# W_Q loaded in eight transfers of 16 rows, and W_O in four pieces with 20 rows summed early

## The chip, the cores and the metric

The kernel runs on one core of a Trainium2 chip. The metric is the device time of one execution in microseconds. An execution is repeated, and the median of the runs is what is compared. The core has five engines that run side by side: TensorE (matrix products; PE in the profile, with its weight loads shown apart as PEld), VectorE (DVE), ScalarE (ACT), GpSimd (POOL) and SyncE (SP), which here only issues transfers. Transfers between DRAM and the on-chip memory of 128 rows are carried by 16 DMA engines. They go through a queue for each issuing engine: `q1` holds what SP issues, `q10` what ScalarE issues.

## The reference

The reference is one decode step of a transformer block in which attention and the feed-forward part are added up. There are four batch rows, one token each, of 512 values; all arrays are bf16.

```python
x  = A_x                                   # [4, 1, 512]
xn = layernorm(x)
# attention: 32 query heads, 8 key/value heads of 128, window = the last 4096 positions
q  = (xn @ wq).reshape(4, 1, 32, 128)      # wq: [512, 4096]
p  = softmax(q . k / sqrt(128))            # k_cache, v_cache: [4, 8, 16384, 128]
a  = (p @ v).reshape(4, 1, 4096) @ wo      # wo: [4096, 512]
# feed-forward part
b  = (silu(xn @ w_gate) * (xn @ w_up)) @ w_down   # 512 -> 1792 -> 512
return x + a + b
```

What has to be read is the keys and values of the window (8 heads of 4 MB each, twice), W_Q and W_O (4 MB each) and the three feed-forward weights (1.8 MB each): 81 MB in all. Each byte is used for four batch rows only.

## The kernel before, in words

**Transfers.** `run_sync` issues all large transfers from SP, in one fixed order: W_Q, W_gate, W_up, the keys of heads 0 and 1, the values of head 0, then in turn the keys of the next head and the values of the one before, the values of head 7, W_down, and W_O. Each has 128 rows on the chip, and each is one transfer, but for W_O, which goes in five pieces. SP stops ahead of a transfer when the buffer it fills is still in use. There are two buffers for keys (`kbuf`) and two for values (`vbuf`). W_Q lies in the second value buffer until the projection is done, W_down in the buffer of W_gate, and W_O in the first key buffer. ScalarE issues the small transfer of x: four rows of 1 KB.

Row p of W_Q on the chip holds the weight rows 4p to 4p+3, which is 32 KB that lie together in DRAM; the same is true of a row of keys or values. Row p of W_O holds the weight rows 32p to 32p+31; a "row" j of W_O in the list `ROWS` is one of these 32, so that a piece of n such rows is n KB on each of the 128 rows of the chip.

**Head of the kernel** (`t_head` in `run_tensor`). TensorE waits for the layernorm and for W_Q (`d_v[1]`, line 469), makes the query projection in 32 products (lines 470 to 476), transposes it, and makes the gate and up projections as soon as their weights are there. The gated product `guT` is kept for the end.

**A pass for each key/value head** (`t_pass`, eight times). TensorE transposes the keys (line 416); VectorE and ScalarE move them to the on-chip memory; TensorE makes the scores (line 425); then come the maximum, the exponential on ScalarE (line 270), the denominators (line 521) and the product with the values (line 434), one head behind.

**The tail** (`t_tail`). The head outputs are normalised and rearranged into `OP`, which VectorE finishes in lines 384 to 389. Meanwhile TensorE sums the feed-forward part, 14 products with W_down, into the four quarters of one bank, `part_ps` (line 572). It then issues idle products: `spin(4)`, line 574, whose result is not used. Then it adds the first `EARLY` rows of W_O to the same four quarters, one product of 512 columns for each (line 582). VectorE and ScalarE copy the bank to the on-chip memory (lines 391 and 273, 64 rows each). A product with `fold` adds the four quarters into two accumulators of 256 columns each (line 587). The other rows of W_O are added straight to these accumulators, two products for each row (line 593). Two copies make `y` (lines 275 and 393), and SP writes it out (line 253).

TensorE waits for each piece of W_O ahead of the first row of it. In the early part there is a `spin(q)` ahead of that wait for piece q: none for piece 0, one idle product for piece 1. An idle product on fp32 operands shows in the trace as two records of line 442.

What sets the order around the change is the program order on each engine and the semaphores. `d_v[1]` counts the transfers into the second value buffer, W_Q first among them, and later waits count on from there.

Of the kernel before, what the change touches and what calls it, by code (L numbers as in the profile page):

```python
# [10 lines left out]
def bass_parallel_sum__sliding_block_cached__swiglu_ffn__decode_kernel(  # L11
# [31 lines left out]
    SCALE = float(Dh) ** -0.5  # L43
    EPS = 1e-5
    BIG = 1.0e30
    ROWS = [(0, 16), (16, 22), (22, 29), (29, 31), (31, 32)]
    EARLY = 22

    sb = nc.alloc_sbuf_tensor
    sb("pad_to_512", [128, (-nc.sbuf_base) % 512 // 2], BF16)  # L50
# [6 lines left out]
    WQ = VB[1][:].rearrange("p t d -> p (t d)").rearrange("p (c n) -> p c n", c=NC)  # L57
# [66 lines left out]
    def sem(name):  # L124
        return nc.alloc_semaphore(name=name)

    d_x = sem("d_x")
    d_k = [sem("d_k%d" % g) for g in range(2)]
    d_v = [sem("d_v%d" % g) for g in range(2)]
    d_wg = sem("d_wg")  # L130
    d_wu = sem("d_wu")
    d_wd = sem("d_wd")
    d_wo = [sem("d_wo%d" % q) for q in range(len(ROWS))]
    d_out = sem("d_out")
# [42 lines left out]
    wq_ap = A_wq.rearrange("(p c) n -> p c n", c=NC)  # L177
# [7 lines left out]
    def kv_ap(cache, r):  # L185
        return cache[:, r, Sk - W:, :].rearrange("b (s t) d -> s b (t d)", t=NT)

    def bc(ap, n):
        return ap.unsqueeze(1).to_broadcast([ap.shape[0], n, ap.shape[1]])
# [36 lines left out]
    def run_sync(eng):  # L226
        def load_k(r):
            if r >= 2:
                eng.wait_ge(s_tr[NCH - 1], r - 1)
            eng.dma_start(KB[r % 2][:].rearrange("p t d -> p (t d)"), kv_ap(A_k_cache, r)).then_inc(d_k[r % 2], 16)  # L230

        def load_v(r):
            if r:
                eng.wait_ge(s_pv, r)
            eng.dma_start(VB[r % 2][:].rearrange("p t d -> p (t d)"), kv_ap(A_v_cache, r)).then_inc(d_v[r % 2], 16)

        eng.dma_start(WQ[:], wq_ap).then_inc(d_v[1], 16)
        eng.dma_start(WG[:], wg_ap).then_inc(d_wg, 16)
        eng.dma_start(WU[:], wu_ap).then_inc(d_wu, 16)
        load_k(0)  # L240
        load_k(1)
        load_v(0)
        for r in range(2, HKV):
            load_k(r)
            load_v(r - 1)
        load_v(HKV - 1)
        eng.dma_start(WD, wd_ap).then_inc(d_wd, 16)
        for q, (a, b) in enumerate(ROWS):
            if q == 0:
                eng.wait_ge(s_tr[NCH - 1], HKV - 1)  # L250
            eng.dma_start(WO[:, a:b, :], wo_ap[:, a:b, :]).then_inc(d_wo[q], 16)
        eng.wait_ge(s_y, 2)
        eng.dma_start(out_ap, y[:]).then_inc(d_out, 16)
        eng.wait_ge(d_out, 16)
# [140 lines left out]
    def run_tensor(eng):  # L395
# [9 lines left out]
        def step(reg, by, op=ALU.add):  # L405
            nc.regs_alu(reg, reg, by, op=op)
# [32 lines left out]
        def spin(n):  # L439

            for _ in range(n):
                mm(spin_ps, identf[:], bc(o4[:], 2), start=True, stop=True)  # L442
# [13 lines left out]
        with nc.body("t_head", valid_engines=me):  # L456
            loc = eng.mark_branch_hint_location()
            for t, v in ((nx, 1), (odd, 0), (nk[0], 16), (nk[1], 16)):
                nc.regs_mov(t, v)
            eng.wait_ge(s_c2, 1)  # L460
            eng.wait_ge(s_xn, 1)
            for c in range(NC):
                last = eng.transpose(xT_ps[:, c * B:(c + 1) * B],  # L463
                                     xn[:].rearrange("b (p c) -> b c p", c=NC)[:, c, :], ident[0:B, 0:B])
            last.then_inc(s_xT, 1)
            eng.wait_ge(s_const, 1)
            mm(mask_ps, Lsel[:], Dsh[:])
            eng.wait_ge(s_xnT, 1)
            eng.wait_ge(d_v[1], 16)
            for c in range(NC):  # L470
                for j in range(2):
                    for k in range(4):
                        last = mm(ps_S[j][32 * k:32 * k + 32, :], XnT[:, c, :],  # L473
                                  WQ[:, c, 512 * (4 * j + k):512 * (4 * j + k) + 512],
                                  start=(c == 0), stop=(c == NC - 1), skip_group_check=True)
            last.then_inc(s_q, 1)
            eng.wait_ge(s_qs, 2)
            for j in range(2):
                for h in range(4):
                    last = eng.transpose(qT_ps[:, 4 * j + h, :], qs[:, j, 128 * h:128 * h + 128], ident[:])  # L480
            last.then_inc(s_qt, 1)
            for w, d, o, s_w in ((WG, d_wg, gate_ps, s_g), (WU, d_wu, up_ps, s_u)):
                wt = w[:].rearrange("p c (m t) -> p c t m", t=NF)
                eng.wait_ge(d, 16)
                for c in range(NC):
                    for k in range(4):
                        last = mm(o[32 * k:32 * k + 32, :].rearrange("p (t m) -> p t m", m=128), XnT[:, c, :],
                                  wt[:, c, T0[k]:T0[k] + 4, :], start=(c == 0), stop=(c == NC - 1), skip_group_check=True)
                last.then_inc(s_w, 1)
            eng.wait_ge(s_gu, 1)  # L490
            for t in range(4):
                last = eng.transpose(gT_ps[:, t, :], gu[:, 128 * t:128 * t + 128], ident[:])
            last.then_inc(s_gt, 1)
            eng.wait_ge(s_qc, 1)
            eng.wait_ge(s_guT, 1)
            nc.br("t_pass", engines=me)
# [63 lines left out]
        with nc.body("t_tail", valid_engines=me):  # L560
            eng.wait_ge(s_nm, LAST + 2)
            eng.transpose(rt_ps, OT[:, 1:, :].rearrange("p r c -> p (r c)"), ident[:]).then_inc(s_rt, 1)
            eng.wait_ge(s_rn, 1)
            for b in range(B):
                m = mm(op_ps[:, b].rearrange("p q j -> p (q j)"), sel[:, b, :], Rn[:], start=(b == 0), stop=True,
                       skip_group_check=True)
            m.then_inc(s_op, 1)
            eng.wait_ge(s_guT, 1)
            eng.wait_ge(d_wd, 16)
            for t in range(NF):  # L570
                k = (t + 1) % 4
                mm(part_ps[32 * k:32 * k + 32, :], guT[:, t, :], WD[:, t, :], start=(t < 3), stop=False,  # L572
                   skip_group_check=True)
            spin(4)
            eng.wait_ge(s_opc, 1)
            for j in range(EARLY):
                for q, (a, b) in enumerate(ROWS):
                    if a == j:
                        spin(q)
                        eng.wait_ge(d_wo[q], 16)  # L580
                k = (j + 3) % 4
                m = mm(part_ps[32 * k:32 * k + 32, :], OP[:, j, :], WO[:, j, :], start=False,  # L582
                       stop=(j >= EARLY - 4), skip_group_check=True)
            m.then_inc(s_pt, 1)
            eng.wait_ge(s_ptc, 2)
            for h in range(2):
                mm(acc_ps[h], fold[:], part[:, 256 * h:256 * h + 256], start=True, stop=False, skip_group_check=True)
            for j in range(EARLY, 32):
                for q, (a, b) in enumerate(ROWS):
                    if a == j:  # L590
                        eng.wait_ge(d_wo[q], 16)
                for h in range(2):
                    m = mm(acc_ps[h], OP[:, j, :], WO[:, j, 256 * h:256 * h + 256],  # L593
                           start=False, stop=(j == 31), skip_group_check=True)
            m.then_inc(s_acc, 1)
            step(seen, 1)
            eng.br_lt(seen, 1, on_true="t_tail", on_false="t_end").branch_hint(loc)
        nc.switch_bb("t_end")

    run_gpsimd(nc.gpsimd)  # L600
    run_sync(nc.sync)
    run_scalar(nc.scalar)
    run_vector(nc.vector)
    run_tensor(nc.tensor)


# [26 lines left out]
```

## Time and profile before

| | |
|---|---|
| median of 3 runs | 196.24 us (196.23 to 196.3) |
| the profiled execution's own time | 196.33 us |
| its span, first to last instruction | 195.0 us |
| moved by DMA | 81.09 MB, mean 416 GB/s |
| busy share of TensorE / VectorE / ScalarE | 81% / 59% / 35% |
| mean granted TensorE clock | 0.965 |

The page gives the share of the span in which each engine was busy, and a row of digits with the busy share in each of 40 slices (4.9 us each). The line "DMA" does the same for the 16 DMA engines together, and "GB/s" gives what they moved. The chain of waits is followed back from the last instruction, each step to what released it. A view by windows gives, for any stretch of time, the busy time of each engine, the granted clock, the share of DMA and the rate. In it the time and the bytes of a packet are put down to the window in which it begins, so that in a short window the share can be over 1. One packet is one row of a transfer, or the few bytes that report the end of one DMA engine's part.

### The profile page before, as it was taken

The numbers are of one execution on the slowest core, as the hardware profiler recorded it, in microseconds if no ns is written. First come the engines' busy times: TensorE is split into PE (matmuls) and PEld (weight loads), VectorE is DVE, ScalarE is ACT, GpSimd is POOL, SyncE is SP. The second block draws the span as 40 slices with busy tenths as digits, with TensorE's granted clock in tenths as the row PEclk, the third lists the DMA queues.
The fourth block names the chain that finished last, engine by engine and source line by source line (L and its number), as shares of the span: only waits on it lengthen the run. The fifth ranks groups of instructions, "written<-read, shape, count | busy, mean of one in ns | idle before, by whom it ended". The sixth has DMA issues, their size and how long they took to land.

```text
span 195.0 us, 6476 instructions
## 1 busy us (share of the span) xinstructions
PE 158.2 (81%) x2889; PEld 123.0 (63%) x2898; DVE 115.5 (59%) x220; ACT 69.2 (35%) x87; POOL 8.8 (5%) x26
## 2 busy tenths in 40 slices
PE   0038945998998899899989986998799849989994
PEld 0013105986787788778778865986588549866532
DVE  4832283667667586766758673667486717674402
ACT  2003100470664357056434704470466034704001
POOL 7910000000000000000000000000000000000000
PEclk9999995899999999999999999799999978999999
DMA  6999999999999999999999999999999999998991
GB/s 229 437 424 426 440 450 437 434 437 434 420 427 423 445 423 444 430 430 430 430 430 430 430 430 430 430 430 430 444 430 430 430 430 430 430 437 376 431 401 70
DMA packets 3621, 81.09 MB, mean 416 GB/s; under 512 B 408, under 2 KB 544, under 8 KB 928
## 3 DMA queue, kind: packets, MB, share of 16 engines
q1 hardware_dynamic: 3608, 81.01, 97.2%
q8 instruction: 4, 0.07, 0.1%
q14 instruction: 1, 0.01, 0.0%
q10 hardware_dynamic: 8, 0.00, 0.0%
HBM read 81.01 MB, written 0.00 MB: 415 GB/s over the span
## 4 chain that ended last, share of the span: by engine, by line
PE 43%; DMA 42%; ACT 8%; DVE 3%; issue 2%; SPq 1%; DVEq 0%; ACTq 0%
DMA kbuf<-in_A_k_cache_dram 42%; PE ps_kt L416 20%; PE ps_s L425 8%; ACT kT L267 7%; PE ps_o L434 5%; PE ps_kt L442 2%; PE ps_s L538 2%; DVE mxb L340 1%; ACT p L270 1%; PE ps_s L582 1%; PE ps_kt L525 1%; PE ps_o L542 1%; PE ps_s L593 1%; DVE mx L363 1%; PE ps_s L572 0%
## 5 line engine op out<-in xcount | busy, mean ns | idle before, releaser
L416 PE MATMUL ps_kt<-ident,kbuf 128*128 128x128 bf16 x1024 | 72.9, 229 | 11.9 <-DMA kbuf<-in_A_k_cache_dram 8.1
L416 PEld LDWEIGHTS ps_kt<-ident,kbuf 128*128 128x128 bf16 x1024 | 62.8, 103 | 18.9 <-DMA kbuf<-in_A_k_cache_dram 8.5
L336 DVE COPY kT<-ps_kt 128x1024 bf16<-128x1024 bf16 x80 | 52.3, 688 | 23.2 <-PE ps_kt L416 22.6
L267 ACT COPY kT<-ps_kt 128x1024 bf16<-128x1024 bf16 x48 | 47.8, 1013 | 47.4 <-PE ps_kt L416 47.4
L270 ACT ACTIVATE p<-ps_s 128x512 bf16<-128x512 f32 x32 | 16.5, 603 | 43.8 <-PE ps_s L538 43.8
L340 DVE TENSOR_REDUCE mxb<-ps_s 128x16 f32<-128x512 f32 x32 | 22.1, 692 | 13.2 <-PE ps_s L425 11.6
L425 PE MATMUL ps_s<-qT,kT 128*128 x1024 | 29.5, 170 | 0.0
L425 PEld LDWEIGHTS ps_s<-qT,kT 128*128 128x128 bf16 x1024 | 27.9, 96 | 0.3
L434 PE MATMUL ps_o<-vbuf,p 128*32 128x256 bf16 x576 | 17.4, 273 | 0.6
L434 PEld LDWEIGHTS ps_o<-vbuf,p 128*32 128x32 bf16 x576 | 15.0, 97 | 2.1 <-issue 1.8
L538 PE MATMUL ps_s<-dsh,lsel 128*128 128x512 bf16 x36 | 9.4, 382 | 0.0
L521 PE MATMUL ps_kt<-p,ones 128*128 128x512 bf16 x27 | 7.6, 379 | 0.9 <-ACT p L270 0.2
L473 PE MATMUL ps_s<-vbuf,xnT 128*32 128x512 bf16 x32 | 3.6, 629 | 5.5 <-DMA vbuf<-in_A_wq_dram 5.5
L344 DVE TENSOR_REDUCE dsum<-ps_kt 128x16 f32<-128x512 f32 x9 | 6.2, 692 | 1.5 <-PE ps_kt L521 1.3
L350 DVE TENSOR_TENSOR oT<-ps_o,rden 128x16 f32 (+1 forms) x9 | 1.6, 175 | 8.9 <-PE ps_o L542 8.9
L525 PEld LDWEIGHTS ps_kt<-identf,mxd 128*128 128x128 f32 x9 | 1.3, 139 | 8.4 <-DVEq L366 8.4
L525 PE MATMUL ps_kt<-identf,mxd 128*128 128x128 f32 x9 | 2.9, 323 | 4.5 <-DVEq L366 4.5
L542 PEld LDWEIGHTS ps_o<-fold,o 128*128 128x128 f32 x36 | 5.4, 191 | 1.3
L463 PE MATMUL ps_s<-ident,xn 4*128 4x4 bf16 x4 | 0.3, 166 | 7.1 <-DVE xn L298 7.1
L473 PEld LDWEIGHTS ps_s<-vbuf,xnT 128*32 128x32 bf16 x32 | 1.2, 138 | 7.0 <-issue 7.0
L538 PEld LDWEIGHTS ps_s<-dsh,lsel 128*128 128x128 bf16 x36 | 2.8, 97 | 4.1 <-issue 1.9
L273 ACT COPY part<-ps_s 64x512 f32<-64x512 f32 x1 | 0.6, 580 | 12.2 <-PE ps_s L582 12.2
(94 smaller groups left out, 81.2 us busy)
## 6 DMA issues: line engine op xcount, KB each, us to landing
kbuf<-in_A_k_cache_dram SPq DMA_DIRECT2D x8, 4096.0 KB, 26.3
vbuf<-in_A_v_cache_dram SPq DMA_DIRECT2D x8, 4096.0 KB, 28.4
vbuf<-in_A_wq_dram SPq DMA_DIRECT2D x1, 4096.0 KB, 12.3
kbuf<-in_A_wo_dram SPq DMA_DIRECT2D x1, 2048.0 KB, 31.3
wg_sb<-in_B_w_gate_dram SPq DMA_DIRECT2D x1, 1792.0 KB, 16.1
wu_sb<-in_B_w_up_dram SPq DMA_DIRECT2D x1, 1792.0 KB, 19.9
wg_sb<-in_B_w_down_dram SPq DMA_DIRECT2D x1, 1792.0 KB, 27.0
kbuf<-in_A_wo_dram SPq DMA_DIRECT2D x1, 896.0 KB, 34.4
```

The source lines that it names most:

```text
L267: eng.copy(KT[n % 8][:], kt_ps[n % 3]).then_inc(s_ev[n], 1)
L270: eng.activation(P[:, q * TB:(q + 1) * TB, :], S_ps[q], ACT.Exp, scale=SCALE).then_inc(s_xp[q], 1)
L336: eng.tensor_copy(KT[n % 8][:], kt_ps[n % 3]).then_inc(s_ev[n], 1)
L340: eng.tensor_reduce(mxb[:, q, :], S_ps[q].rearrange("p t c -> p c t"), AX.X, ALU.max)
L344: eng.tensor_reduce(dsum[:], dn_ps[:].rearrange("p (t c) -> p c t", c=CQ), AX.X, ALU.add)
L416: last = eng.transpose(kt_ps[n % 3][:, k, :], KB[g][:, 8 * n + k, :], ident[:])
L425: last = mm(S_ps[q][:, 8 * (n % 4) + k, :], KT[n % 8][:, k, :], QT[:, bass.ds(j, 1), :, :].rearrange("p o b h -> p (o b h)"), start=(n % 4 ...
L434: last = mm(o4_ps[32 * k:32 * k + 32, :], P[:, 2 * u:2 * u + 2, :].rearrange("p t c -> p (t c)"), VB[e][:, 2 * u:2 * u + 2, :].rearrange(" ...
L521: last = mm(dn_ps[:], ones[:], P[:, q * TB:(q + 1) * TB, :].rearrange("p t c -> p (t c)"), start=(q == 0), stop=(q == NB - 1))
L525: eng.transpose(mx_ps, mxd[:], identf[:]).then_inc(s_mt, 1)
L538: mm(S_ps[q], Lsel[:], bc(Dsh[:], TB), start=False, stop=True, skip_group_check=True).then_inc(s_sh[q], 1)
L542: last = mm(ot_ps, o4[:, 128 * e:128 * e + 128], fold[:, 16 * e:16 * e + 16], start=(e == 0), stop=(e == 1), skip_group_check=True)
```

## The change

W_Q goes in eight transfers of 16 chip rows each instead of one of 128. The first seven report to a semaphore of their own, `d_wq`, the last to `d_v[1]`, as the single one did. The projection waits for both. W_O goes in four pieces of 20, 8, 3 and 1 rows instead of five of 16, 6, 7, 2 and 1. The early part ends after 20 rows instead of 22, so 20 rows are summed in the four quarters and 12, not 10, go straight to the accumulators. The `spin(q)` in the early part is gone; with the old list it was one idle product, ahead of the second piece.

```diff
-    ROWS = [(0, 16), (16, 22), (22, 29), (29, 31), (31, 32)]
-    EARLY = 22
+    ROWS = [(0, 20), (20, 28), (28, 31), (31, 32)]
+    EARLY = 20
...
+    d_wq = sem("d_wq")
...
-        eng.dma_start(WQ[:], wq_ap).then_inc(d_v[1], 16)
+
+        for a in range(0, 128, 16):
+            eng.dma_start(WQ[a:a + 16], wq_ap[a:a + 16]).then_inc(d_wq if a < 112 else d_v[1], 16)
...
             eng.wait_ge(s_xnT, 1)
+            eng.wait_ge(d_wq, 112)
             eng.wait_ge(d_v[1], 16)
...
                 for q, (a, b) in enumerate(ROWS):
                     if a == j:
-                        spin(q)
                         eng.wait_ge(d_wo[q], 16)
```

## The prediction

> **What bounds the kernel now.** I read the page first, its slices and its queues.
>
> ```profile
> span 195.0 us, 6476 instructions
> ...
> DMA  6999999999999999999999999999999999998991
> GB/s 229 437 424 426 440 450 437 434 437 434 420 427 423 445 423 444 430 430 430 430 430 430 430 430 430 430 430 430 444 430 430 430 430 430 430 437 376 431 401 70
> ...
> q1 hardware_dynamic: 3608, 81.01, 97.2%
> ...
> q10 hardware_dynamic: 8, 0.00, 0.0%
> ```
>
> The DMA engines have work from the first slice to the last but one, at 430 GB/s. At that rate 81.01 MB take 188.4 us of a span of 195.0. So the kernel is one stream of transfers, with compute beside it. Then the issues and the tail of TensorE, in order of time:
>
> ```profile
> 0.73 0.41 SPq L237 DMA_DIRECT2D vbuf<-in_A_wq_dram  x1
> 1.20 0.41 SPq L238 DMA_DIRECT2D wg_sb<-in_B_w_gate_dram  x1
> ...
> 3.43 0.62 SPq L235 DMA_DIRECT2D vbuf<-in_A_v_cache_dram  x1
> ...
> 13.12 3.60 PE L473 MATMUL ps_s<-vbuf,xnT 128*32 128x512 bf16 x32 [5.50 <-DMA vbuf<-in_A_wq_dram]
> ...
> 31.36 3.92 PE L416 MATMUL ps_kt<-ident,kbuf 128*128 128x128 bf16 x35 [2.40 <-DMA kbuf<-in_A_k_cache_dram]
> ...
> 156.46 2.33 SPq L251 DMA_DIRECT2D kbuf<-in_A_wo_dram  x5
> ```
> ```profile
> 184.53 3.63 PE ps_kt L442 x8
> 188.16 0.98 PE ps_s L582 x16
> 189.13 1.06 PE ps_kt L442 x2
> 190.19 0.56 PE ps_s L582 x6
> 190.75 0.02 issue
> 190.77 0.69 DVE part L391
> 191.46 0.04 issue
> 191.51 0.62 PE ps_s L587 x4
> 192.13 1.11 PE ps_s L593 x20
> 193.24 0.02 issue
> ```
> ```profile
> kbuf<-in_A_wo_dram SPq DMA_DIRECT2D x1, 2048.0 KB, 31.3
> ...
> kbuf<-in_A_wo_dram SPq DMA_DIRECT2D x1, 896.0 KB, 34.4
> kbuf<-in_A_wo_dram SPq DMA_DIRECT2D x1, 768.0 KB, 32.7
> kbuf<-in_A_wo_dram SPq DMA_DIRECT2D x1, 256.0 KB, 34.6
> kbuf<-in_A_wo_dram SPq DMA_DIRECT2D x1, 128.0 KB, 34.5
> ```
>
> The five issues of W_O are 2.33/5 = 0.47 us apart, so the pieces land at 156.46 + 31.3 = 187.8, 189.6, 191.8, 192.5 and 192.9. The first product that reads the last piece starts at about 193.1. W_O was issued 31 us before it landed: it waits behind other transfers, and what delays the stream anywhere ahead delays it in full. Idle time of the DMA engines that could take up a delay is at most 195.0 - 188.4 = 6.6 us, and of that 1.8 us lie ahead of the first row and 2 us behind the last.
>
> **W_Q in eight transfers.** How are rows dealt out? q1 has 25 transfers of 128 rows, and 25 × (128 + 16) + 8 = 3608: one packet for a row and 16 that report the end, one for each DMA engine; the 8 are the output's four rows. q10's 8 are x alone: 4 rows of 1 KB and 4 reports, so four rows go to four engines. A transfer of 16 rows therefore goes to 16 engines, one row each, and an engine carries 8 rows of 32 KB of W_Q, as before. What differs is which rows are written at one time: 16 neighbours instead of rows from all over the 128.
>
> The only neighbouring rows written together in this trace are x's. Windows around them (columns: window, its length, five engines, clock, DMA share, GB/s):
>
> ```profile
> 1.69:1.71 0.02, 0.00 (x0) 0.00 (x0) 0.00 (x0) 0.02 (x1) 0.02 (x1) 1.00 0.14 51
> 1.71:1.73 0.02, 0.00 (x0) 0.00 (x0) 0.00 (x0) 0.02 (x1) 0.02 (x2) 1.00 0.24 51
> 1.75:1.75 0.01, 0.00 (x0) 0.00 (x0) 0.00 (x0) 0.01 (x1) 0.01 (x2) 1.00 0.49 102
> 2.20:2.24 0.04, 0.00 (x0) 0.00 (x0) 0.00 (x0) 0.04 (x1) 0.00 (x0) 1.00 0.07 26
> ...
> 1.76:1.92 0.16, 0.00 (x0) 0.00 (x0) 0.00 (x0) 0.16 (x1) 0.16 (x4) 1.00 6.10 1608
> ...
> 1.76:3.60 1.84, 0.00 (x0) 0.00 (x0) 0.85 (x3) 0.85 (x1) 1.30 (x8) 1.00 0.99 286
> 4.84:6.06 1.22, 0.00 (x0) 0.00 (x0) 0.83 (x3) 0.20 (x1) 1.03 (x3) 1.00 1.00 430
> 10.86:12.07 1.21, 0.00 (x0) 0.00 (x0) 0.57 (x3) 0.00 (x0) 0.00 (x0) 1.00 1.00 433
> 12.07:16.30 4.23, 3.17 (x32) 1.24 (x32) 0.00 (x0) 0.00 (x0) 0.00 (x0) 1.00 1.01 430
> ```
>
> Rate times length is 1.02 KB in each of the first four: one row of x each. Share × 16 × length is its time: 0.045, 0.077, 0.078 and 0.045 us (the third window is 0.01 us long). The first row, and the fourth, begun when the others were over, take 0.045. The second and the third begin while the row before them is on its way, and take 0.03 us more: what is left of their predecessor. That is how rows look that go one after another although four engines carry them. A second reading is open: the four also lie together in DRAM (4 KB), and could have queued there.
>
> For W_Q the row 4.84:6.06 gives 430 × 1.22 = 525 KB, 16 rows of 32 KB, in 1.22 us: eight such rounds are 9.8 us. If four neighbours go one after another, a round of 16 rows takes 4 × 1.22 = 4.88 us, which is 3.66 more, and eight rounds 29.3 more. The lower end is nothing: engines that have drifted a row apart no longer meet. Between them decides how fast they drift. Row 1.76:1.92 has 1608 × 0.16 = 257 KB, so eight engines begin W_Q within 0.16 us, 0.02 apart. Where one of four finishes a row ahead by some work, the other three share the way for three times that while it has its next rows to itself: a lead triples in each round. From 0.02 us it needs five rounds to reach 0.02 × 3^5 = 4.9 us, a whole round; the slowest of a group, which sets the end, stays in step for six to eight. I take seven: 7 × 3.66 = **+25.6 us**; six give 22.0 and eight 29.3.
>
> [...] The x rows agree with sharing; no run shown here measures its rate.
>
> Who carries the delay: all other transfers stand behind W_Q on the same 16 engines, so W_gate, W_up, keys and values land later by as much. TensorE already waits for W_Q (5.50 us) and for the first keys (2.40). It cannot make the time up, because the last transfers end the kernel.
>
> **SP and the new wait.** Seven more issues of 0.41 us, 0.47 apart, move W_gate's issue from 1.20 to 4.5 and the values' from 3.43 to 6.7. The engines are busy with W_Q until 12.07 at least, which hides it: 0; uncovered, 3.3 us. The wait on `d_wq` holds the 32 products of line 473 and all that follows on TensorE, but each engine reports its first seven rows before its eighth: 0, or one of the chain's 0.05 us steps. Whether each of eight transfers has a pause at its start: the first round (1.76:3.60) took 1.84 us for its 526 KB where the later ones need 1.22, so 0.6 at the start; between W_Q and W_gate (10.86:12.07, then 12.07:16.30) the rate stays at 433 and 430, so a new transfer in the queue costs nothing. I take 0; the bounds are -0.6 (the first round becomes as fast as the others) and +7 × 0.6 = +4.3 (each starts like the first).
>
> **The tail.** One row of W_O is 131 KB, 0.305 us at 430 GB/s. The first piece, four rows longer, lands at 187.8 + 1.22 = 189.0. TensorE ends `spin(4)` at 188.16, waits 0.85, then makes 20 products at 0.98/16 = 0.061: 190.25, where it was 190.75. The removed idle product held 1.06 us (L442 x2 at 189.13); the piece it waited beside had landed at 189.6, so the six products behind it began 0.6 late. Copies and steps take 0.76, the `fold` products 0.62: 191.6. Rows 20 to 27 land by 191.5; 16 products at 1.11/20 = 0.056 end at 192.5. Rows 28 to 30 land at 192.5, six products, 192.85; row 31 lands at 192.85, two products, 193.0. The last product ended at 193.24: **-0.25 us**. Then the last landing is what ends it. The wait of 0.85 replaces idle work, so the clock could fall. It did fall behind longer waits:
>
> ```profile
> 29.30:34.10 4.80, 2.74 (x26) 2.74 (x27) 1.54 (x4) 0.00 (x0) 0.00 (x0) 0.50 0.95 410
> ```
>
> That follows idle stretches of which the last is the 2.40 us before the first keys. I take full clock for 0.85; half clock would add 1.2 us on the 20 products.
>
> **Sum.** Against the profiled execution's 196.33 us (span 195.0 and 1.3 around it, 0.09 above the median of 196.24): 196.33 + 25.6 - 0.25 = 221.7; by the median 221.6. With six to eight rounds and the bounds of the small terms the likeliest case's own range is 217 to 226.
>
> **The rivals.**
>
> *Not slower: neighbours don't wait for each other on the chip.* x's rows then queued in DRAM, where W_Q's, 32 KB each, needn't. Each piece gives every engine one row at once, so the 0.6 us of the first round may go, and the tail gives 0.25: 196.33 - 0.25 - 0 to 0.6 = 195.5 to 196.1, middle 195.8. It decides if the second 16 rows of W_Q run at over 400 GB/s. For it: 430 GB/s hold wherever 16 engines work, as if an engine were the limit. Against it: the times of x's second and third row. That the transfers would not run as written, but each on the four engines near its rows, ends here too, since eight such pieces would run side by side; x, with four rows begun within 0.06 us on engines of their own, speaks against that.
>
> *Half as bad:* two of four can be written at a time. A round takes 2.44 us: 196.33 + 9.8 - 0.25 = 205.9. The 0.077 of x's rows is 1.7 times 0.045, but it is explained by a late start; little else speaks for this.
>
> *Each piece starts anew,* 0.6 us for each: 196.33 + 4.3 - 0.25 = 200.4, or some part of it, 197 to 200. The steady 433 and 430 GB/s across the boundary speak against it.
>
> **Chances.** Forecast 0.60, no waiting 0.28, half 0.06, starting anew 0.06. Less than 0.2% (0.4 us) can't be told from no change here. Slower holds the forecast and two rivals, less a small start: 0.70. The no-waiting case gives faster by over 0.4 us (under 195.84) with 0.19 and no change with 0.09; a small start adds 0.02 to no change. The range must reach down to that case to leave out no more than 2 in 10: 195.6 to 226.
>
> **What would show it.** W_Q issued eight times, the last landing near 38 us instead of 13; windows between 3 and 30 at 105 to 150 GB/s with the DMA share still near 1.0, because waiting rows count as busy; the first product of line 473 at 38 to 39, the first of line 416 at 57; from there each pass as before. In the tail, no L442 between products of line 582, one wait for W_O ahead of 20 of them, and 24 records of line 593. I am wrong if the slices of the first 15 us stay at 430 GB/s; then the tail alone decides. The tail's step is wrong if the last product starts over 0.3 us behind the last landing.

## The result, and the profile after

The changed kernel takes 222.43 us (median of 6 runs, 222.16 to 222.54), the one before 196.27 us (6 runs, 196.16 to 196.41). The ratio is 1.133, with a 95% interval of 1.131 to 1.134: 26.2 us slower. The forecast was 221.6.

The page of the changed kernel, span, slices and queues:

```profile
span 220.8 us, 6482 instructions
...
DMA  9988993999999999998999999999999999999993
GB/s 125 160 95 95 113 172 52 434 464 404 451 412 436 448 404 460 393 463 386 469 398 463 404 451 427 427 457 398 463 392 469 398 463 398 457 427 400 441 399 123
...
q1 hardware_dynamic: 3576, 81.01, 97.7%
```

A slice is now 5.5 us. In the first six the DMA engines count as busy (8 or 9 tenths), yet they move only 95 to 172 GB/s; in the seventh, with 3 tenths and 52 GB/s, few rows begin. From the eighth slice on the stream is what it was. The 3576 packets of q1 are 23 × (128 + 16) + 8 × (16 + 16) + 8: each piece of W_Q is 16 rows and 16 reports, one row for each engine, as the prediction took it. The loss lies wholly in the first 39 us. The issues and the first products, in order of time:

```profile
0.73 3.68 SPq L240 DMA_DIRECT2D vbuf<-in_A_wq_dram  x8
...
4.46 0.42 SPq L241 DMA_DIRECT2D wg_sb<-in_B_w_gate_dram  x1
...
6.70 0.60 SPq L236 DMA_DIRECT2D vbuf<-in_A_v_cache_dram  x1
...
39.14 3.29 PE L477 MATMUL ps_s<-vbuf,xnT 128*32 128x512 bf16 x32 [31.23 <-DMA vbuf<-in_A_wq_dram]
...
57.27 4.98 PE L419 MATMUL ps_kt<-ident,kbuf 128*128 128x128 bf16 x45 [3.02 <-DMA kbuf<-in_A_k_cache_dram]
```

The first product with W_Q starts at 39.14 us where it was 13.12, 26.0 later, and the first transposed keys at 57.27 where they were 31.36, 25.9 later. What W_Q lost stays lost to the end. The same stretch by windows (columns: window, its length, five engines, clock, DMA share, GB/s):

```profile
1.72:1.73 0.01, 0.00 (x0) 0.00 (x0) 0.00 (x0) 0.01 (x1) 0.01 (x1) 1.00 0.28 102
1.73:1.74 0.01, 0.00 (x0) 0.00 (x0) 0.00 (x0) 0.01 (x1) 0.01 (x2) 1.00 0.28 102
...
4.90:9.40 4.50, 0.46 (x5) 0.31 (x5) 3.25 (x6) 0.20 (x1) 4.09 (x6) 1.00 1.00 117
9.40:13.90 4.50, 0.00 (x0) 0.00 (x0) 2.29 (x5) 0.00 (x0) 1.47 (x3) 1.00 1.01 117
...
27.40:31.90 4.50, 0.00 (x0) 0.00 (x0) 0.00 (x0) 0.00 (x0) 0.00 (x0) 1.00 1.01 117
```

117 GB/s over 4.50 us are some 526 KB: one transfer of 16 rows (16 × 32 KB). A row that took 1.22 us takes 4.50. Eight times the difference is 26.2 us.

The tail, the chain of waits of the changed kernel:

```profile
182.45 32.48 DMA kbuf<-in_A_wo_dram
214.93 0.14 issue
215.06 1.29 PE ps_s L585 x20
216.35 0.02 issue
216.37 0.69 DVE part L394
217.07 0.04 issue
217.11 0.63 PE ps_s L590 x4
217.74 1.35 PE ps_s L596 x24
```

TensorE now waits for the first piece of W_O; after that the chain has no wait on W_O up to the end of the last product at 219.09. In this execution the tail won little: 219.09 less the 26.0 of W_Q is 193.1, against 193.24 before.

### The profile page after: what moved, and what is told of

The parts are those of the page before. It is cut to its first block, busy times and chain, and to the rows that moved or that the text cites. A ratio compares the mean times of both kernels' runs of the same rounds, so it can differ in the third digit from the quotient of the medians.

```text
span 220.8 us, 6482 instructions
## 1 busy us (share of the span) xinstructions
PE 155.4 (70%) x2889; PEld 121.1 (55%) x2898; DVE 115.6 (52%) x220; ACT 69.2 (31%) x87; POOL 9.1 (4%) x26
## 3 DMA queue, kind: packets, MB, share of 16 engines
q1 hardware_dynamic: 3576, 81.01, 97.7%
## 4 chain that ended last, share of the span: by engine, by line
DMA 43%; PE 39%; DVE 6%; ACT 6%; SPq 2%; issue 2%; another core or an unknown queue 1%; DVEq 0%
PE ps_kt L419 18%; DMA vbuf<-in_A_wq_dram 16%; DMA kbuf<-in_A_wo_dram 15%; DMA kbuf<-in_A_k_cache_dram 13%; PE ps_s L428 8%; ACT kT L270 6%; PE ps_o L437 4%; PE ps_s L542 2%; PE ps_s L491 2%; DVE mxb L343 2%; DVE kT L322 2%; PE ps_s L477 2%; SPq L240 1%; PE ps_kt L529 1%
## 5 line engine op out<-in xcount | busy, mean ns | idle before, releaser
L419 PE MATMUL ps_kt<-ident,kbuf 128*128 128x128 bf16 x1024 | 72.0, 227 | 13.6 <-DMA kbuf<-in_A_k_cache_dram 9.8
L419 PEld LDWEIGHTS ps_kt<-ident,kbuf 128*128 128x128 bf16 x1024 | 61.6, 102 | 20.9 <-DMA kbuf<-in_A_k_cache_dram 10.3
L264 ACT CAST kT<-ps_s 128x512 bf16<-128x512 f32 x1 | 0.6, 585 | 36.9 <-PE ps_s L477 36.9
```

The source lines that it names most:

```text
L419: last = eng.transpose(kt_ps[n % 3][:, k, :], KB[g][:, 8 * n + k, :], ident[:])
```

## The experiments

**The parts one by one.** Two kernels change the tail alone, one W_Q alone, and one cuts W_Q into eight in another direction. The tail alone:

```diff
-    ROWS = [(0, 16), (16, 22), (22, 29), (29, 31), (31, 32)]
-    EARLY = 22
+    ROWS = [(0, 20), (20, 28), (28, 31), (31, 32)]
+    EARLY = 20
...
-                        spin(q)
```

> The kernel before with the new tail alone: W_O in four pieces of 20, 8, 3 and 1 rows, 20 of them in the four quarters, no idle product between; W_Q in one transfer. My sum gives -0.25 us, 196.0. The trace of the changed kernel gives -0.16, since its last product ended 219.09 where the delay of W_Q (39.00 against 12.99 us for the last report) put the old end at 219.25: 196.1. The rival: the last landing ends both tails and nothing is won, 196.3.

Measured: 196.28 us against 196.39 of the kernel before in the same series, ratio 1.0002 (0.998 to 1.002). The difference can't be told from no change. The chain of waits of this run shows why so little is left, beside its issues of W_O and the landing of its last piece:

```profile
156.74 32.48 DMA kbuf<-in_A_wo_dram
189.23 0.14 issue
189.36 1.29 PE ps_s L581 x20
...
192.03 1.36 PE ps_s L592 x24
193.39 0.02 issue
```
```profile
156.74 1.85 SPq L251 DMA_DIRECT2D kbuf<-in_A_wo_dram  x4
```
```profile
kbuf<-in_A_wo_dram SPq DMA_DIRECT2D x1, 128.0 KB, 34.9
```

The fourth issue is at 156.74 + 3 × 0.46 = 158.1, so the last piece lands at 193.0, and the last product ends, at 193.39, 0.35 later; before, it was 192.85 and 0.4. Both tails end with the last landing and a few tenths.

Only the idle product taken out, five pieces as before:

```diff
-                        spin(q)
                         eng.wait_ge(d_wo[q], 16)
```

> The kernel before without the one idle product ahead of the second piece of W_O; five pieces as before. If that product held up the six products behind it by 0.6 us, the last product ends at about 193.0 instead of 193.24, -0.2 us: 196.05. If the last landing (192.8) ends the tail anyway: 196.25.

Measured: 196.52 us, ratio 1.0016 (1.0002 to 1.003): not faster. The six products behind the idle one were late, but not what ended the kernel; the chain of this run ends on a landing of W_O and the 20 last products:

```profile
157.35 34.40 DMA kbuf<-in_A_wo_dram
191.75 0.04 issue
191.80 1.32 PE ps_s L592 x20
```

W_Q in eight transfers of 16 rows, with the tail as before:

```diff
-        eng.dma_start(WQ[:], wq_ap).then_inc(d_v[1], 16)
+        for a in range(0, 128, 16):
+            eng.dma_start(WQ[a:a + 16], wq_ap[a:a + 16]).then_inc(d_wq if a < 112 else d_v[1], 16)
```

> W_Q in eight transfers of 16 rows alone; the tail as before. If W_Q makes all of the loss and the new tail gains a little: 196.27 + 26.2 + 0.2 = 222.6. If the tail has a part in the loss: under 222.0.

Measured: 222.65 us, ratio 1.133 (1.131 to 1.135). This part makes the whole loss.

W_Q in eight transfers that each take all 128 rows and an eighth of the columns:

```diff
-        eng.dma_start(WQ[:], wq_ap).then_inc(d_v[1], 16)
+        for a in range(8):
+            c, h = a // 2, 2048 * (a % 2)
+            eng.dma_start(WQ[:, c, h:h + 2048], wq_ap[:, c, h:h + 2048]).then_inc(d_wq if a < 7 else d_v[1], 16)
```

> W_Q in eight transfers too, but each takes all 128 chip rows and an eighth of the columns (4 KB of each row). If the place of the rows on the chip makes the loss: no change but for small pieces, 196.2 to 196.8. If the number of transfers, of issues or of reports makes it (each piece starts anew): 200 to 222.

Measured: 196.88 us, ratio 1.0027 (1.0009 to 1.0046): 0.5 us for seven more transfers, issues and sets of reports and for rows cut to 4 KB. The first product with W_Q starts at 13.38 us:

```profile
13.38 3.29 PE L477 MATMUL ps_s<-vbuf,xnT 128*32 128x512 bf16 x32 [5.47 <-DMA vbuf<-in_A_wq_dram]
```

So the loss comes from which rows a transfer takes, not from how many transfers there are.

**Chip rows or DRAM rows.** A transfer of 16 neighbouring chip rows also reads 512 KB that lie together in DRAM. Two kernels part the two. The first fills neighbouring chip rows from far DRAM rows:

```diff
+        for a in range(8):
+            eng.dma_start(WQ[16 * a:16 * a + 16], wq_ap[a:128:8]).then_inc(d_wq if a < 7 else d_v[1], 16)
```

> As the eight transfers of 16 neighbouring chip rows, but what fills them is taken from DRAM rows that lie 8 apart (256 KB) instead of together. Each chip row then holds another row's weights, and the result is not the reference's; the work is the same. If the chip rows make the loss: 222.5, a row 4.5 us. If it comes from 16 engines reading 512 KB that lie together in DRAM: 196 to 200, a row 1.22 us.

Measured: 223.46 us (two runs, 221.87 and 225.05), with rows at the slow pace:

```profile
9.40:14.00 4.60, 0.00 (x0) 0.00 (x0) 2.35 (x5) 0.00 (x0) 1.54 (x3) 1.00 1.00 114
```

The second puts DRAM rows that lie together on chip rows 8 apart:

```diff
+        for a in range(8):
+            eng.dma_start(WQ[a:128:8], wq_ap[16 * a:16 * a + 16]).then_inc(d_wq if a < 7 else d_v[1], 16)
```

> The reverse: eight transfers of 16 rows that lie together in DRAM and go to chip rows 8 apart. Rows hold other rows' weights here too. If only four neighbours share a way: 196.3, a row 1.22 us. If rows 32 apart share too, the 16 rows use 8 ways, two engines on each: 204.6, a row 2.25 us. If the loss comes from DRAM, or if an engine is slow wherever it writes away from its usual rows: 222.5.

Measured: 206.52 us, ratio 1.052 (1.049 to 1.055), with 16 rows in 2.52 us:

```profile
13.88:16.40 2.52, 0.00 (x0) 0.00 (x0) 0.00 (x0) 0.00 (x0) 0.00 (x0) 1.00 1.01 208
```

The DRAM side plays no part that shows (223.46 us here, 222.65 with the rows together in DRAM); the chip rows do. And "four neighbours" isn't the whole of it, as no two of these rows are neighbours, yet 16 of them take 2.52 us instead of 1.22. Some rows that lie 8 or a multiple of 8 apart must hold each other up too. This run doesn't say which: that rows 32 apart share, and that there are 8 ways, were the author's assumptions.

**How many rows share.** W_Q in four transfers of 32 rows and in two of 64:

```diff
+        for a in range(0, 128, 32):   # and 64 in the other kernel
+            eng.dma_start(WQ[a:a + 32], wq_ap[a:a + 32]).then_inc(d_wq if a < 96 else d_v[1], 16)
```

> W_Q in four transfers of 32 neighbouring rows, tail as before. Each engine carries two rows of each, so four neighbours belong to two engines. If engines at the same four rows share one way: a row takes half of the 4.5 us that it takes in the changed kernel, 2.25 instead of 1.22, +8.3 us, 204.6. If each engine is slow by itself whenever it writes away from its usual rows: 4.5 us, 222. [...]

> W_Q in two transfers of 64 neighbouring rows, tail as before. Each engine has four neighbours to itself, so if only neighbours share a way nothing is lost: 196.3. [...]

Measured: 206.71 us with 32 rows (ratio 1.053, 1.050 to 1.056) and 207.09 with 64 (1.055, 1.052 to 1.058). One window of each:

```profile
8.57:11.14 2.57, 0.00 (x0) 0.00 (x0) 2.54 (x3) 0.00 (x0) 2.33 (x3) 1.00 1.00 204
```
```profile
14.00:16.58 2.58, 0.00 (x0) 0.00 (x0) 0.00 (x0) 0.00 (x0) 0.00 (x0) 1.00 1.00 203
```

Both are 524 KB, 16 rows, in 2.57 or 2.58 us. An engine that is slow by itself away from its usual rows would have given 222 in the first of them. With 64 rows and four to an engine, as I took the rows to be dealt out, no two engines write the same four neighbours, yet the run lost 10.8 us; so rows further off hold each other up as well. The four cases, 16 neighbours, 32 rows, 64 rows and 16 rows 8 apart, run at 117, 204, 203 and 208 GB/s, against 430 for 128 rows. Which rows share a way, and how many ways there are, isn't shown by any run.

**Does a lead help?** In my prediction an engine that gets ahead finds free ways and gets further ahead. The windows of the changed kernel say no: 117 GB/s from 4.90 to 31.90, without a change. Narrower windows show when the rows of the second round begin, and those of the eighth:

```profile
4.94:6.05 1.11, 0.00 (x0) 0.00 (x0) 0.69 (x4) 0.20 (x1) 0.90 (x3) 1.00 4.07 472
6.05:9.42 3.37, 0.46 (x5) 0.31 (x5) 2.55 (x3) 0.00 (x0) 3.22 (x4) 1.00 0.00 0
...
31.94:33.06 1.12, 0.00 (x0) 0.00 (x0) 0.00 (x0) 0.00 (x0) 0.00 (x0) 1.00 4.06 468
33.06:36.44 3.38, 0.00 (x0) 0.00 (x0) 0.00 (x0) 0.00 (x0) 0.00 (x0) 1.00 0.00 0
```

472 × 1.11 is 524 KB, all 16 rows of the round; in the 3.37 us behind, none begins. Six rounds later the 16 starts take 1.12 us. So the engines stayed as far apart as they were, and no lead grew. To test larger leads, two pairs of kernels put an extra transfer of 8 rows of 16 KB into an unused tile ahead of W_Q, which was to hold up 8 of the 16 engines. In the first pair it goes first of all:

```diff
+    scr = sb("scr", [8, 8192], BF16)
...
+        eng.dma_start(scr[:], wo_ap[0:8, 0:16, :].rearrange("p j n -> p (j n)")).then_inc(d_scr, 16)
         # then W_Q: one transfer, or two of 64 rows
```

> The kernel before, with an extra transfer of 8 rows of 16 KB ahead of W_Q, into a tile that nothing reads. It occupies 8 of the 16 engines and puts them behind the others. Eight neighbours use two ways of four engines each, so it takes half of the changed kernel's 4.5 us for 32 KB, 2.25 us, and the end moves by that: 198.6. If an engine alone sets the speed, 0.6 us: 196.9.

> The same extra transfer, then W_Q in two transfers of 64 rows, where the engines of the two halves share ways in pairs. The rows that the profile gives never drift apart; this gives one half of the engines a start of about 2.25 us. If engines that are out of step really use free ways (my prediction's step: a lead grows), the leaders have the first half of the rows to themselves, are on the second half when the others are alone on the first, and the last row ends after 17.8 us instead of 20.6 + 2.25: 196.3 + 17.8 - 9.7 = 204.4. If a lead is of no use, because the engines are held to one pace: 206.9 + 2.3 = 209.2.

Measured: 197.65 us (ratio 1.008, 1.0001 to 1.015) and 208.48 us (1.061, 1.057 to 1.065), against 196.64. The lag alone is 1.0 us (with a wide interval, 0.0 to 3.0), the 64 rows alone 10.8; together they cost 11.8, the sum. The two ways of four engines each for eight neighbours, and with them the 2.25 us, were the author's estimate; no run shows them. And the extra transfer did not part the engines. In the run with 64 rows, the second rows of W_Q begin like this:

```profile
5.60:6.17 0.57, 0.00 (x0) 0.00 (x0) 0.22 (x3) 0.20 (x1) 0.57 (x2) 1.00 4.53 920
6.17:8.17 2.00, 0.46 (x5) 0.31 (x5) 1.56 (x3) 0.00 (x0) 1.85 (x3) 1.00 0.00 0
```

920 × 0.57 is 524 KB again, all 16 rows, and none follows in the next 2.00 us. No half of the engines is 1 to 2.25 us ahead: all 16 were held up, and they start closer together than without the extra transfer, where these starts take 1.42 us (369 GB/s from 3.96 to 5.38). The second pair puts W_gate ahead, so that the lag comes when the engines run steadily:

```diff
+        eng.dma_start(WG[:], wg_ap).then_inc(d_wg, 16)
+        eng.dma_start(scr[:], wo_ap[0:8, 0:16, :].rearrange("p j n -> p (j n)")).then_inc(d_scr, 16)
         # then W_Q
```

> As the run with the extra transfer of 8 rows and W_Q in one transfer, but W_gate goes first, so that the extra transfer comes when the engines run steadily and its lag isn't lost in the slow first round. If four engines share a way: 16 KB at the pace of 4.5 us for 32 KB, 2.25 us of lag, 198.6; the run before had 1.3 us of it, 197.6.

> The same with W_Q in two transfers of 64 rows: half of the engines now come to it with a start of 1.3 to 2.25 us. If engines that are out of step use free ways, W_Q needs 17.8 us from the leaders' start instead of 9.7: 196.3 + 8.1 = 204.4, or up to 205.7 with the smaller start. If all are held to one pace: the 10.4 of the run with 64 rows and the lag, 208 to 209.4.

Measured: 199.0 us (1.014, 1.011 to 1.017) and 209.63 us (1.068, 1.065 to 1.071), against 196.36: a lag of 2.6 us alone, 13.3 with the 64 rows, where 2.6 + 10.8 is 13.4. Again the sum, and not the 204 to 206 of a lead that is used. The windows of the last kernel, the first and the last around the starts of the second and the eighth row:

```profile
9.93:12.13 2.20, 0.00 (x0) 0.00 (x0) 0.76 (x3) 0.00 (x0) 0.74 (x1) 1.00 1.16 238
15.00:17.58 2.58, 0.00 (x0) 0.00 (x0) 0.00 (x0) 0.00 (x0) 0.00 (x0) 1.00 0.99 203
17.58:19.95 2.37, 0.00 (x0) 0.00 (x0) 0.00 (x0) 0.00 (x0) 0.00 (x0) 1.00 1.02 221
20.00:22.60 2.60, 0.00 (x0) 0.00 (x0) 0.00 (x0) 0.00 (x0) 0.00 (x0) 1.00 0.99 202
25.07:27.34 2.27, 0.00 (x0) 0.00 (x0) 0.00 (x0) 0.00 (x0) 0.00 (x0) 1.00 1.15 231
```

Here the 16 second rows begin within 2.20 us, and the eighth within 2.27: the engines are further apart than without the extra transfer, they stay so, and the pace is the old one. The shorter round in the middle (221 GB/s) is no gain from a lead, since the run with 64 rows alone has it too, 225 GB/s from 11.68 to 14.01. But 2.20 us is the distance from the first engine to the last, not a lead of one half over the other. With W_Q in one transfer, too, all 16 second rows begin within 0.92 us (570 GB/s from 9.83 to 10.75) and none in the 0.75 us before, so that again all engines were held up, and not 8. The 131 KB of the extra transfer would take 0.3 us at 430 GB/s and cost 2.6. What a lead of half of the engines does is therefore not tested by either pair. Why an extra transfer to 8 rows holds up all engines, and why engines on different rows keep to one pace, isn't shown by any run.

## Why the prediction was right, and where it was not

**The bound.** Right. The delay of W_Q's first product and the change of the time go together: 26.0 and 26.2 us in the changed one, 10.4 and 10.4 with 32 rows, 10.7 and 10.8 with 64, 10.1 and 10.2 with rows 8 apart. The stream has no slack that takes any of it up.

**W_Q, the mechanism.** Neighbouring chip rows that are written together hold each other up: right (16 of them take 4.50 us, 16 of the 128 took 1.22), and shown to lie with the chip rows by parting them from the DRAM rows (223.46 us with the DRAM rows apart, 206.52 with the chip rows apart). That four neighbours share one way in was the author's estimate; no run shows that number. The evidence that the prediction had for the sharing was wrong. It read x's rows as waiting for one another (0.077 us instead of 0.045 when they overlap). In the changed kernel two of x's rows, begun within 0.02 us, take 0.28 × 16 × 0.01 = 0.045 us each (windows 1.72 and 1.73 above). These 1 KB rows don't show the sharing; what made two of them slow before is open. So nothing in the trace of before bore the sharing out.

**W_Q, the size.** +25.6 was forecast, 26.2 came, and the nearness is partly luck. A round of 16 rows was put at 4 × 1.22 = 4.88, with a factor of four that no run shows; the runs showed 4.50, 3.7 times 1.22. And the step "a lead triples in each round", which left seven of eight rounds in step, failed: the 16 starts of the second round took 1.11 us from first to last, those of the eighth 1.12, and all eight rounds went at the slow pace. 7 × 3.66 and 8 × 3.28 happen to lie 0.6 apart.

**SP and the new wait.** W_gate was issued at 4.46 (4.5 was forecast), the values at 6.70 (6.7), and neither shows. A price for each transfer was put at 0, with bounds from -0.6 to +4.3; cut by columns it is 0.5 us for seven more.

**The tail.** -0.25 was forecast; alone the new tail shows no change (ratio 1.0002, though the interval, -0.3 to +0.4 us, doesn't exclude -0.25). The step that failed is the end behind the last landing. The sum let the last product end 0.15 us after it (192.85 and 193.0), where it had been 0.4 before; all of the -0.25 lies there. In the run with the tail alone it is 0.35 us, and without the idle product 0.34 (192.78 and 193.12), where the last 20 products begin at a landing, too. The sum took two products at their spacing of 0.056 us; in the profile one of them takes 0.27 from its start to its modelled end (median of line 592 in the run with the tail alone). The 20 products were mis-sized as well: 1.25 us after the landing of the first piece by the sum, 1.42 in that run (189.23 to 190.65), 0.14 of it between the report and the first product. So the new tail ends a few tenths behind the last landing, as the old one did. The full clock that was assumed through the 0.85 us wait is what the changed kernel's window shows:

```profile
215.06:219.10 4.04, 3.22 (x48) 1.75 (x48) 0.68 (x1) 0.58 (x1) 0.00 (x0) 1.00 0.46 178
```

**The rivals.** "Neighbours don't wait for each other" falls with the 117 GB/s. "Half as bad" is what 32 and 64 rows do, at 206.7 and 207.1 where that rival said 205.9. "Each piece starts anew" falls with the eight transfers by columns.

## What to carry to other kernels

If a large load has to be cut, cut it along the columns so that each transfer still covers all 128 chip rows: eight such pieces cost 0.5 us here, eight pieces of 16 rows 26. A DMA share near 1.0 doesn't say that bytes move; read it beside the rate (1.00 at 117 GB/s in the changed kernel, 1.00 at 430 in the one before). In a kernel like this, whose stream of transfers never runs dry, an early loss comes out at the end in full (26.0 us at W_Q, 26.2 in the time), and a tail that ends with the last landing isn't shortened by taking work out of it (196.28 and 196.52 us against 196.39).

## What the runs showed of the hardware that was not expected

- At half the pace (32 rows, 64 rows, or 16 rows 8 apart) a row of 32 KB takes 2.52 to 2.58 us in the windows shown, more than twice 1.22; with 16 neighbours it takes 4.50, less than four times.
- The slow pace of the changed kernel stayed at 117 GB/s from 4.90 to 31.90 us, and engines that were apart stayed so: starts 1.11 us apart in the second round and 1.12 in the eighth of the changed kernel, 2.20 and 2.27 in the last one.
- An extra transfer of 131 KB to 8 chip rows, put in a running stream, held up all 16 engines and cost 2.6 us (199.0 against 196.36).
- TensorE's first 32 products with W_Q were slow in three kernels with different waits ahead of them: 3.60 us after 5.50 us without work (the kernel before), 3.29 after 5.47 (eight transfers by columns) and 3.29 after 31.23 (the changed kernel). That is at least 0.10 each, where 16 products of the same form took 0.98 in the tail, 0.06 each. The window gives a granted clock of 1.00, but the first record of the clock in this trace begins at 42.0 us, so it doesn't say whether the clock was the reason:

```profile
38.00:43.00 5.00, 3.29 (x32) 1.24 (x32) 0.52 (x2) 0.52 (x1) 0.00 (x0) 1.00 0.91 381
```
